# Splitting an output product around the end of its attention block: an adaptive-norm transformer block on one core

## The chip, the cores and the metric

The kernel runs on one core of a Trainium2 chip. The metric is the device time of one launch in microseconds (us). A core has five engines with a queue of instructions each, worked off in order: TensorE (PE in the profile; PEld is its weight load), VectorE (DVE), ScalarE (ACT), GpSimd (POOL) and SyncE (SP), which here issues all DMAs.

## The reference

One transformer block with conditioned norms on 2048 rows of 512: a modulation row from a condition vector, full softmax attention with 32 heads of 16, and a feed-forward part of width 1792 with the Mish function.

```python
mod = (_silu(c) @ w_mod).reshape(c.shape[0], 6, 1, -1)
sa, ca, ga, sb, cb, gb = (mod[:, 0], mod[:, 1], mod[:, 2], mod[:, 3], mod[:, 4], mod[:, 5])
h = _layernorm(x, axis=-1) * (1 + ca) + sa
x = x + ga * _A_ref(h, A_wqkv, A_wo)      # attention: softmax(q k^T / 4) v, then @ wo
h = _layernorm(x, axis=-1) * (1 + cb) + sb
x = x + gb * _B_ref(h, B_w1, B_b1, B_w2)  # mish(h @ w1 + b1) @ w2
return x
```

Everything is fp32. Operands of the large products are held as a rounded high part and a low part ("h" and "l"), and a product is three products (high x high, high x low, low x high) summed in one bank.

## The kernel before

The rows are cut into 4 blocks of 512 queries (`NB`), the heads into 8 groups of 4 (`G`); an iteration `n` is one group of one block, 32 in all, and it has 16 *steps*, so the loop has `T` = 512 steps. The code counts in half steps `h` (two to a step); `at(h, f)` puts work at a half step, and each engine's instructions are then issued in that order. Nothing is scheduled on the chip: a late engine makes those that wait for it late.

In a step TensorE makes four score tiles (keys x queries, L513, whose exponential ScalarE takes at L521), four tiles for the row maxima of an iteration 20 steps ahead (L472, reduced by VectorE at L474), and the product of the exponentials with the values (L541, eight records a step). Scores and maxima use one half of TensorE's rows at a time, and beside them, in the other half, run products of other work in *slots*: at first the q, k, v projections, later the MLP. Each such product is done in two halves, in the even and the odd step of a pair. `next_part` takes the next *unit* from the list `units` at an even step, if its time `ready` has come; 6 slots go into a step pair, so a unit of 12 takes two pairs (8 half steps) and one of 6 takes one pair (4 half steps). In the last 20 steps, which have no maxima, 3 slots go into a pair's step. A unit accumulates in the one bank `ms`; its `fin` evicts it.

The row maxima of a group go through `max_rows` (L485 on): transposed, negated into `mt` by ScalarE (L494), reduced to their rounded rows `mh` by GpSimd (L495), subtracted by GpSimd (L496), and written by DMA beside the queries, where the score product subtracts them.

When the 8 groups of a block are through (the last one's rows are normalized by GpSimd at L587 and split at L96 and L99 into `o_hl`), the block's MLP work starts, beside the next block's attention. For blocks 0 to 2 the queue is, in this order (`all_blocks`): the last down units of the block before, the output product `wo` of the four row tiles (12 slots each, not before half step `t0` = 256 (qb + 1) + 14), the norm (`norm_y`) and the transposes of the four tiles (`tr_unit`, a *special* that is put at a step's end), and 14 `up` units (the first MLP product with `mish` behind it, 12 slots) mixed with `down` units (the second MLP product, in 5 groups of 2, 4, 4, 2 and 2 of the 14 slices, each for 4 row tiles, 6 or 12 slots). Block 0 can only begin when the projections are through and the MLP's memory is open.

After an output product ScalarE copies the bank into `yd` (L824; one buffer), GpSimd adds it to the rows `y`, which hold x (L825), ScalarE sums the rows for the mean (L702), takes the squares (L706), and GpSimd makes the norm (L703 to L709). `tr_unit` evicts the transposed tile with ScalarE (L851), scales it with GpSimd (L854) and splits it into `hx` (L96, L99). `down` units evict in the same way (L896, L897).

Block 3 has no attention to hide behind: `tail` does its MLP alone, with full-height products. The third block's last ten down units are held back (`mst["held"]`) and fill TensorE in the tail while the last rows are normed on VectorE (L1023 to L110) and transposed (L1045). Their additions to y are VectorE's (L893).

```python
for js in ((0, 1), (2, 3)):
    for f in held(js):
        f(None)
...
fins = held((4, 5))
```

Of the kernel before, what the change touches and what calls it, by code (L numbers as in the profile page):

```python
# [18 lines left out]
def adaln_block(ctx: ExitStack, tc: tile.TileContext, x, wqkv, wo, w1, b1, w2, c, w_mod, out):  # L19
    nc = tc.nc  # L20
# [60 lines left out]
    nc.vector.tensor_scalar_mul(lows[:32], lows[:32], -1.0)  # L81
    modc = cst.tile([P, 4, DK], F32, name="modc")
    sil = cst.tile([P, DK], F32, name="sil")
# [227 lines left out]
    with ExitStack() as es:  # L311
# [36 lines left out]
        def stats_tb(tb):  # L348

            mv = lp.tile([P, 4, 2], F32, tag="ln_mv4", name="ln_mv4", bufs=2)  # L350
            rs = rss[tb] = lp.tile([P, 4, 4], F32, tag="ln_rs4", name="ln_rs4", bufs=3)
# [5 lines left out]
            nc.gpsimd.tensor_scalar(rs[:, 3, :], mv[:, :, 0], -1.0, 0.0, op0=ALU.mult, op1=ALU.add)  # L357
            nc.gpsimd.tensor_tensor(rs[:, 1, :], rs[:, 0, :], nhalf.to_broadcast([P, 4]), op=ALU.pow)
            nc.gpsimd.tensor_mul(rs[:, 2, :], rs[:, 3, :], rs[:, 1, :])
# [126 lines left out]
    def max_rows(n, mm):  # L486
        t = ring(2)
        cols = mm.rearrange("p a v q -> p (a v q)")
        for g in range(2):
            r = slice(64 * g, 64 * g + 64)  # L490
            nc.tensor.transpose(t[:32, g, :64], cols[r], ident[r, r])
        mh, mt = [ap.tile([32, P], F32R, tag=n_, name=n_, bufs=1) for n_ in ("mh", "mt")]
        mc = mt.bitcast(F32)
        nc.scalar.activation(mc.rearrange("p (g q) -> p g q", g=2), t[:32, :, :64], AF.Copy, scale=-1.0)  # L494
        nc.gpsimd.tensor_scalar_mul(mh, mc, lows[:32])  # L495
# [200 lines left out]
    def norm_y(y):  # L696
        mp = mst["p"]
        xn = mp.tile([P, D], F32, tag="hb", name="xn2", bufs=3)
        ss = mp.tile([P, 4], F32, tag="ln_s", name="ln_s", bufs=4)

        def mean():
            nc.scalar.activation(xn, y, AF.Identity, accum_out=ss[:, 0:1])  # L702
            nc.gpsimd.tensor_scalar(ss[:, 1:2], ss[:, 0:1], -1.0 / D, 0.0, op0=ALU.mult, op1=ALU.add)  # L703

        def spread():
            nc.scalar.activation(xn, y, AF.Square, bias=ss[:, 1:2], accum_out=ss[:, 2:3])  # L706
            nc.gpsimd.tensor_scalar(ss[:, 2:3], ss[:, 2:3], 1.0 / D, EPS, op0=ALU.mult, op1=ALU.add)
            nc.gpsimd.tensor_tensor(ss[:, 3:4], ss[:, 2:3], nhalf, op=ALU.pow)
            nc.gpsimd.tensor_scalar(xn, y, ss[:, 1:2], ss[:, 3:4], op0=ALU.add, op1=ALU.mult)  # L709

        return xn, mean, spread
# [85 lines left out]
    def block(qb, t0):  # L797

        xn, y, act, w1s, w2s, wos, done, hx = {}, {}, {}, {}, {}, {}, {}, []
# [14 lines left out]
        def wo_unit(i, tag):  # L814
# [3 lines left out]
            seq = [(l[:, k, s], wos[k][:, v, :]) for k in range(DK) for l, v in ((oh, 0), (oh, 1), (ol, 0))]  # L818
# [3 lines left out]
            def fin(h):  # L822
                yd = mst["p"].tile([P, D], F32, tag="yd", name="yd", bufs=1)
                nc.scalar.copy(yd, acc)  # L824
                nc.gpsimd.tensor_add(y[i], yd, y[i])  # L825

                def mean():
                    xn[i], first, then = norm_y(y[i])
                    first()
                    at(h + 5, then)  # L830

                at(h + 3, mean)
                done["xn", i] = h + 7
# [47 lines left out]
        def down_unit(gi, i, tag=None, acc=None):  # L881
# [9 lines left out]
            def fin(h):  # L891
# [24 lines left out]
                if then and (gi, i) == (4, 0):  # L916
                    load(h + 20, then["y"], lambda j: load_y(qb + 1, j), range(3, 4))
# [3 lines left out]

        def wo(i):
            queue(lambda: max(t0, done.get("w", 0 if qb else 4 * T)), lambda tag: wo_unit(i, tag))
            queue_special(lambda: done.get(("xn", i), 4 * T), lambda: tr_unit(i))
# [9 lines left out]
        if qb == NB - 2:  # L934
            mst["held"] = lambda j, acc: down_unit(2 + (j + 2) // 4, (j + 2) % 4, None, acc)
        return {"wo": wos, "y": y, "w1": w1s, "w2": w2s, "loads": first_loads,
                "units": {"wo": wo, "up": up, "down": down}}

    def all_blocks():
# [3 lines left out]
        for qb, b in enumerate(blocks):  # L943
            wo, up, down = (b["units"][k] for k in ("wo", "up", "down"))
            before = blocks[qb - 1]["units"]["down"] if qb else lambda gi, i: None
            before(4, 0)
            for i in range(4):
                wo(i)
# [17 lines left out]
            up(13)  # L966
            if qb < NB - 2:
                down(2, 2)
                down(2, 3)
# [24 lines left out]
    def tail():  # L994
# [46 lines left out]
        fins = held((4, 5))  # L1041
# [8 lines left out]
        for js in ((6, 7), (8, 9)):  # L1050
# [329 lines left out]
```

## Time and profile before

| | us |
|---|---|
| median of 3 runs (lowest, highest) | 1688.13 (1687.86, 1689.64) |
| the profiled execution's own time | 1686.03 |
| its span, first to last instruction | 1684.2 |
| TensorE busy | 1655.4 |
| VectorE busy | 1427.3 |
| ScalarE busy | 1327.9 |
| GpSimd busy | 928.3 |

Busy times are sums over the span, and the engines work at the same time. The rows of the profile name a line, an engine, an operation, what it writes and reads, how often it comes, then busy time and mean duration in ns, then idle time in front of it and who ended that. The timeline's rows begin with start and duration in us; the bracket is idle time in front and its releaser. The granted clock of TensorE was 0.998 over the span.

### The profile page before, as it was taken

The numbers are of one execution on the slowest core, as the hardware profiler recorded it, in microseconds if no ns is written. First come the engines' busy times: TensorE is split into PE (matmuls) and PEld (weight loads), VectorE is DVE, ScalarE is ACT, GpSimd is POOL, SyncE is SP. The second block draws the span as 40 slices with busy tenths as digits, with TensorE's granted clock in tenths as the row PEclk, the third lists the DMA queues.
The fourth block names the chain that finished last, engine by engine and source line by source line (L and its number), as shares of the span: only waits on it lengthen the run. The fifth ranks groups of instructions, "written<-read, shape, count | busy, mean of one in ns | idle before, by whom it ended". The sixth has DMA issues, their size and how long they took to land.

```text
span 1684.2 us, 33102 instructions
## 1 busy us (share of the span) xinstructions
PE 1655.4 (98%) x12316; PEld 925.5 (55%) x12316; DVE 1427.3 (85%) x2330; ACT 1327.9 (79%) x2591; POOL 928.3 (55%) x970
## 2 busy tenths in 40 slices
PE   7999999999999999999999999999999999999999
PEld 5755665555435455555555555555555555554687
DVE  6898898888898888888888888888888888882577
ACT  6257777787778889888889898888888888889364
POOL 5156225465435398854535498654535597645532
PEclk9999999999999999999999999999999999999999
DMA  7777456777784343435343644334442644232362
GB/s 256 191 221 213 123 158 195 236 227 218 213 249 113 107 107 86 119 78 161 87 122 75 199 104 97 102 108 118 122 102 59 189 103 133 80 122 83 126 225 75
DMA packets 113993, 240.04 MB, mean 143 GB/s; under 512 B 24048, under 2 KB 49648, under 8 KB 107784
## 3 DMA queue, kind: packets, MB, share of 16 engines
q1 hardware_dynamic: 113832, 237.92, 50.1%
q8 instruction: 97, 1.59, 0.4%
q14 instruction: 64, 0.52, 0.1%
HBM read 179.95 MB, written 51.44 MB: 137 GB/s over the span
## 4 chain that ended last, share of the span: by engine, by line
PE 84%; POOL 5%; DVE 3%; ACT 3%; issue 2%; DMA 2%; SPq 0%; POOLq 0%; ACTq 0%; DVEq 0%
PE bk L541 27%; PE ring L472 22%; PE ring L513 20%; PE bk L133 6%; PE bk L127 3%; PE ring L127 3%; ACT pr L521 2%; PE ring L1078 2%; DVE mx L474 1%; DMA ka<-kscr 1%; POOL rr L775 1%; POOL ee L773 1%; POOL hb L776 1%; POOL ee L743 1%; POOL hb L777 1%
## 5 line engine op out<-in xcount | busy, mean ns | idle before, releaser
L474 DVE TENSOR_REDUCE mx<-ring 128x1 f32<-128x512 f32 x2048 | 1279.2, 684 | 168.4 <-PE bk L133 110.6
L521 ACT ACTIVATE pr<-ring 128x512 f32<-128x512 f32 x2048 | 1088.0, 604 | 210.4 <-PE bk L133 164.4
L472 PE MATMUL ring<-ka,qa 64*128 64x512 f32 x2048 | 775.1, 426 | 1.7 <-DVE mx L474 0.7
L513 PE MATMUL ring<-qa,ka 64*128 64x512 f32 x2048 | 719.4, 395 | 5.7 <-ACT pr L521 5.2
L472 PEld LDWEIGHTS ring<-ka,qa 64*128 64x128 f32 x2048 | 365.9, 184 | 412.8 <-DVE mx L474 354.2
L541 PE MATMUL bk<-pr,vg 128*32 128x512 f32 x4096 | 545.1, 604 | 0.0
L513 PEld LDWEIGHTS ring<-qa,ka 64*128 64x128 f32 x2048 | 374.1, 184 | 112.1 <-ACT pr L521 40.2
L133 PE MATMUL bk<-h,w 64*128 64x512 f32 x1008 | 281.2, 409 | 0.0
L133 PE MATMUL bk<-w,a_h 64*128 64x512 f32 x576 | 194.7, 417 | 2.6 <-ACT pr L521 1.2
L133 PEld LDWEIGHTS bk<-h,w 64*128 64x128 f32 x1008 | 171.6, 184 | 2.4 <-ACT yd L896 0.4
L541 PEld LDWEIGHTS bk<-pr,vg 128*32 128x32 f32 x4096 | 80.9, 108 | 124.7 <-issue 116.7
L133 PE MATMUL bk<-w,a_l 64*128 64x512 f32 x288 | 113.8, 395 | 0.0
L743 POOL TENSOR_SCALAR ee<-hb 128x512 f32<-128x512 f32 x42 | 62.4, 1486 | 91.9 <-ACT hb L737 83.1
L133 PEld LDWEIGHTS bk<-w,a_h 64*128 64x128 f32 x576 | 95.3, 185 | 7.5 <-ACT pr L521 2.4
L773 POOL TENSOR_TENSOR ee<-ee,rr 128x512 f32<-128x512 f32 x42 | 53.8, 1282 | 71.8 <-ACT rr L764 71.6
L133 PE MATMUL bk<-w,o_hl 64*128 64x512 f32 x288 | 79.6, 408 | 0.0
L99 POOL TENSOR_TENSOR a_l<-hb,a_h 128x512 fp32r<-128x512 f32 x53 | 71.6, 1351 | 4.4
L897 POOL TENSOR_TENSOR y<-yd,y 128x512 f32<-128x512 f32 x40 | 51.4, 1286 | 28.2 <-ACT yd L896 28.2
L495 POOL TENSOR_SCALAR mh<-mt,lows 32x128 fp32r<-32x128 f32 x32 | 19.1, 596 | 81.4 <-ACT mt L494 81.2
L133 PE MATMUL bk<-h_h,wl 64*128 64x512 f32 x168 | 56.8, 418 | 0.0
L777 POOL TENSOR_TENSOR hb<-hb,rr 128x512 f32<-128x512 f32 x42 | 54.5, 1298 | 3.3
L758 POOL TENSOR_TENSOR ee<-ee,rr 128x512 f32<-128x512 f32 x42 | 54.0, 1286 | 3.5
(210 smaller groups left out, 1852.5 us busy)
## 6 DMA issues: line engine op xcount, KB each, us to landing
ka<-kscr SPq DMA_DIRECT2D x124, 384.0 KB
w<-w2scr SPq DMA_DIRECT2D x56, 512.0 KB
w<-w1scr SPq DMA_DIRECT2D x46, 512.0 KB
vg<-vscr SPq DMA_DIRECT2D x32, 552.0 KB
qa<-qscr SPq DMA_DIRECT2D x124, 100.0 KB
kscr<-qh SPq DMA_DIRECT2D x16, 512.0 KB
qscr<-qh SPq DMA_DIRECT2D x32, 256.0 KB
w1scr<-hl SPq DMA_DIRECT2D x14, 512.0 KB
```

The source lines that it names most:

```text
L99: (nc.gpsimd if eng == "p" else nc.vector).tensor_sub(lo, src, hi.bitcast(F32))
L127: nc.tensor.matmul(acc, l, r, start=start, stop=stop)
L133: i = nc.tensor.matmul(acc, l[64 * g:64 * g + 64], r[64 * g:64 * g + 64], start=start, stop=stop)
L472: nc.tensor.matmul(pm, qt[64 * s:64 * s + 64, qs * P:(qs + 1) * P], kt[64 * s:64 * s + 64, kb * TB:(kb + 1) * TB], start=True, stop=True)
L474: return nc.vector.tensor_reduce(out=mxs[n][:, s, 4 * j + qs, kb:kb + 1], in_=pm, op=ALU.max, axis=AX.X)
L513: nc.tensor.matmul(p_, kt[64 * s:64 * s + 64, kc * P:(kc + 1) * P], qt[64 * s:64 * s + 64, :], start=True, stop=True)
L521: e = nc.scalar.activation(pr, p_, AF.Exp, scale=SCALE)
L541: nc.tensor.matmul(accs[n][32 * h:32 * h + 32, :], vgs[n][:, o:o + 32], pts.pop((t, h)), start=(kc == 0), stop=(kc == 15))
L743: nc.gpsimd.tensor_scalar_min(buf("ee", 2), b["hb"], HCAP)
L758: nc.gpsimd.tensor_mul(ee, ee, rr)
L773: nc.gpsimd.tensor_mul(ee, ee, rr)
L777: nc.gpsimd.tensor_mul(hb, hb, rr)
```

## The change

The output product of a row tile becomes two units of 6 slots: `part` with the first two of the four slices of the contraction (heads 0 to 15, which are through long before the block's end) and `wo` with the other two. The four parts stand in the queue behind the first of the previous block's last down units and in front of the four `wo`, and need not wait for `t0`. Both halves are copied to `yd` and added to `y`.

The mean of a row is no longer summed over `y`: it is the mean of x, kept from the first norm in `xmean`, plus the two copies' own sums (`accum_out`). The squares come 3 half steps behind the eviction instead of 5.

In `max_rows`, ScalarE makes `mh` from the transposed bank, with a per-partition scale; GpSimd keeps the subtraction.

The third block's down(2,2) and down(2,3) leave the tail for the loop, so that 8 down units are held instead of 10; 5 of them, not 6, stand ahead of the transposes. The fourth row tile's x for the next block is loaded 11 half steps behind down(4,0) instead of 20.

```diff
-        nc.gpsimd.tensor_scalar_mul(mh, mc, lows[:32])
+        nc.scalar.activation(mh.rearrange("p (g q) -> p g q", g=2), t[:32, :, :64], AF.Identity, scale=lows[:32])
         nc.gpsimd.tensor_add(mt, mc, mh.bitcast(F32))
...
-        def mean():
-            nc.scalar.activation(xn, y, AF.Identity, accum_out=ss[:, 0:1])
-            nc.gpsimd.tensor_scalar(ss[:, 1:2], ss[:, 0:1], -1.0 / D, 0.0, op0=ALU.mult, op1=ALU.add)
...
-            seq = [(l[:, k, s], wos[k][:, v, :]) for k in range(DK) for l, v in ((oh, 0), (oh, 1), (ol, 0))]
+            seq = [(l[:, k, s], wos[k][:, v, :]) for k in ks for l, v in ((oh, 0), (oh, 1), (ol, 0))]
...
             def fin(h):
                 yd = mst["p"].tile([P, D], F32, tag="yd", name="yd", bufs=1)
-                nc.scalar.copy(yd, acc)
+                if ks[0] == 0:
+                    ss[i] = mst["p"].tile([P, 4], F32, tag="ln_s", name="ln_s", bufs=4)
+                m, part = (ss[i][:, j:j + 1] for j in ((0, 2) if ks[0] == 0 else (1, 3)))
+                nc.scalar.activation(yd, acc, AF.Identity, accum_out=part)
                 nc.gpsimd.tensor_add(y[i], yd, y[i])
-                def mean():
-                    xn[i], first, then = norm_y(y[i])
-                    first()
-                    at(h + 5, then)
-                at(h + 3, mean)
-                done["xn", i] = h + 7
+                nc.gpsimd.tensor_scalar(m, part, -1.0 / D, 0.0, op0=ALU.mult, op1=ALU.add)
+                if ks[0] == 0:
+                    nc.gpsimd.tensor_add(m, m, xmean[:, 4 * qb + i:4 * qb + i + 1])
+                    return
+                nc.gpsimd.tensor_add(m, m, ss[i][:, 0:1])
+                def spread():
+                    xn[i] = norm_y(y[i], ss[i])
+                at(h + 3, spread)
+                done["xn", i] = h + (7 if i else 5)
...
-                    load(h + 20, then["y"], lambda j: load_y(qb + 1, j), range(3, 4))
+                    load(h + 11, then["y"], lambda j: load_y(qb + 1, j), range(3, 4))
...
+        def part(i):
+            queue(lambda: 0 if qb else done.get("w", 4 * T) + 4, lambda tag: wo_unit(i, tag, range(2)))
+
         def wo(i):
-            queue(lambda: max(t0, done.get("w", 0 if qb else 4 * T)), lambda tag: wo_unit(i, tag))
+            queue(lambda: t0, lambda tag: wo_unit(i, tag, range(2, DK)))
...
-            mst["held"] = lambda j, acc: down_unit(2 + (j + 2) // 4, (j + 2) % 4, None, acc)
+            mst["held"] = lambda j, acc: down_unit(3 + j // 4, j % 4, None, acc)
...
             before(4, 0)
+            for i in range(4):
+                b["units"]["part"](i)
             for i in range(4):
                 wo(i)
...
             up(13)
+            down(2, 2)
+            down(2, 3)
             if qb < NB - 2:
-                down(2, 2)
-                down(2, 3)
...
-        fins = held((4, 5))
+        fins = held((4,))
...
-        for js in ((6, 7), (8, 9)):
+        for js in ((5, 6), (7,)):
```

More of the change, by code (lines that the diff above doesn't have):

```diff
@@ L80, in adaln_block @@
                             axis=AX.XY)
-    nc.vector.tensor_scalar_mul(lows[:32], lows[:32], -1.0)
     modc = cst.tile([P, 4, DK], F32, name="modc")
+    xmean = cst.tile([P, NKC], F32, name="xmean")
     sil = cst.tile([P, DK], F32, name="sil")
@@ L350, in stats_tb @@
             mv = lp.tile([P, 4, 2], F32, tag="ln_mv4", name="ln_mv4", bufs=2)
-            rs = rss[tb] = lp.tile([P, 4, 4], F32, tag="ln_rs4", name="ln_rs4", bufs=3)
+            nm = xmean[:, 4 * tb:4 * tb + 4]
+            rs = rss[tb] = lp.tile([P, 3, 4], F32, tag="ln_rs4", name="ln_rs4", bufs=3)
             for i in range(4):
@@ L694, in load_y, with norm_y @@
         return y
[L696 to L699, printed above, removed]
-        def mean():
[L702 to L711, printed above, removed]
+    def norm_y(y, ss):
+        xn = mst["p"].tile([P, D], F32, tag="hb", name="xn2", bufs=3)
+        nc.scalar.activation(xn, y, AF.Square, bias=ss[:, 1:2], accum_out=ss[:, 2:3])
+        nc.gpsimd.tensor_scalar(ss[:, 2:3], ss[:, 2:3], 1.0 / D, EPS, op0=ALU.mult, op1=ALU.add)
+        nc.gpsimd.tensor_tensor(ss[:, 3:4], ss[:, 2:3], nhalf, op=ALU.pow)
+        nc.gpsimd.tensor_scalar(xn, y, ss[:, 1:2], ss[:, 3:4], op0=ALU.add, op1=ALU.mult)
+        return xn
     def put_h(hh, hl, acc, k, tail):
@@ L797, in block @@
     def block(qb, t0):
-        xn, y, act, w1s, w2s, wos, done, hx = {}, {}, {}, {}, {}, {}, {}, []
+        xn, y, ss, act, w1s, w2s, wos, done, hx = {}, {}, {}, {}, {}, {}, {}, {}, []
         def load(h, d, load_, keys):
@@ L934, in block @@
         if qb == NB - 2:
-            mst["held"] = lambda j, acc: down_unit(2 + (j + 2) // 4, (j + 2) % 4, None, acc)
+            mst["held"] = lambda j, acc: down_unit(3 + j // 4, j % 4, None, acc)
         return {"wo": wos, "y": y, "w1": w1s, "w2": w2s, "loads": first_loads,
-                "units": {"wo": wo, "up": up, "down": down}}
+                "units": {"wo": wo, "part": part, "up": up, "down": down}}
     def all_blocks():
```

6 lines of the change are left out of this document (3 added, 3 removed).

## The prediction

> **What bounds the kernel now.** I read the page first, then TensorE's timeline around a few steps, then a table of stretches, then the groups by line, and at last the timelines of GpSimd, ScalarE and VectorE where a step was longer than its neighbours.
>
> ```profile
> span 1684.2 us, 33102 instructions
> PE 1655.4 (98%) x12316; PEld 925.5 (55%) x12316; DVE 1427.3 (85%) x2330; ACT 1327.9 (79%) x2591; POOL 928.3 (55%) x970
> PE 84%; POOL 5%; DVE 3%; ACT 3%; issue 2%; DMA 2%; SPq 0%; POOLq 0%; ACTq 0%; DVEq 0%
> ```
>
> TensorE is busy nearly always and carries 84% of the chain; GpSimd is the only other engine with a share worth a look. But a busy TensorE is not one price per step. The loop's 512 steps each end with eight records of the values' product (L541), so the starts of two such groups are one step apart:
>
> ```profile
> 457.22 1.06 PE L541 MATMUL bk<-pr,vg 128*32 128x512 f32 x8
> 459.95 1.06 PE L541 MATMUL bk<-pr,vg 128*32 128x512 f32 x8
> ...
> 840.54 1.07 PE L541 MATMUL bk<-pr,vg 128*32 128x512 f32 x8
> 842.62 0.49 PE L133 MATMUL bk<-w,a_h 64*128 64x512 f32 x1 [0.58 <-ACT yd L896]
> 844.52 1.06 PE L541 MATMUL bk<-pr,vg 128*32 128x512 f32 x8
> ```
>
> ```profile
> 457.22:468.17 10.95, 10.29 (x68) 4.07 (x67) 10.14 (x18) 8.38 (x18) 0.88 (x2) 1.00 0.72 256
> 504.37:515.75 11.38, 11.38 (x93) 6.14 (x91) 10.27 (x18) 9.63 (x21) 2.52 (x4) 1.00 0.36 137
> 1528.00:1537.00 9.00, 9.00 (x67) 3.94 (x65) 0.93 (x2) 8.84 (x18) 8.67 (x10) 1.00 0.56 211
> ```
>
> (Columns: stretch, its length, busy time and count on PE, PEld, DVE, ACT, POOL, then clock and DMA.) The first stretch is four steps without MLP products: 10.95 / 4 = 2.74 us, and VectorE is busy 10.14 of it, four maxima of 0.68 us a step. The second is four steps with six products: 11.38 / 4 = 2.845 us, TensorE full. So six product slots, which keep TensorE busy, cost 0.11 us a step as long as VectorE needs 2.74 us anyway. The third stretch lies in the last 20 steps, which have no maxima: ScalarE is busy 8.84 of 9.00 us there, and the steps last about 2.1 us. Above these floors stand a few longer steps, such as 840.54 to 844.52 (3.98 us, 1.14 too long). After the loop comes a tail in which TensorE works alone.
>
> **The tail: two product units less.** By the queue's order (the times follow from the units' lengths, 12 slots two step pairs, 6 slots one), the second block's units follow the first's without a gap, and so do the third's: each block waits neither for its start time nor for the attention, except block 0, which stands idle from half step 232 to 272. There the four first parts take half steps 252 to 268, the second parts end at 288 instead of 304, and everything behind moves forward by 16 half steps, through blocks 1 and 2. At the end this makes room for down(2,2) and down(2,3) of the third block, which end exactly with the loop, in 16 steps at three slots. In the tail these are 24 products fewer:
>
> ```profile
> 1583.77 11.17 PE ring L127 x48
> 1596.68 5.58 PE ring L127 x24
> ```
>
> ```profile
> 1590.26 0.55 DVE L110 TENSOR_SCALAR pr<-pr,ln_mv,ln_rs 128x512 f32<-128x512 f32 x1 [0.72 <-POOL ln_rs L108]
> 1590.72 2.47 DVE L893 TENSOR_TENSOR y<-ring,y 128x512 f32<-128x512 f32 x4
> 1594.77 0.60 PE L1045 MATMUL ring<-ident,pr 128*128 128x128 f32 x4
> ```
>
> One product is 11.17 / 48 = 0.233 us, so 24 are 5.6 us. But the 48 before the transposes (L1045) also covered the norm of the last rows, which ends at 1590.8 (L110). Now there are 30, which end at 1583.4 + 7.0 = 1590.4. The first transposes take the bank that VectorE's first y addition frees, at about 1590.72 + 0.68 = 1591.4: one microsecond of wait appears, of which the 18 products behind the transposes (4.2 us against 5.6) hide what the splits of h need. I take 0.7 us back: **-4.9 us**, bounds -5.6 (all) and -3.8.
>
> In the last 20 steps the slots are free, since ScalarE sets them. The price in the loop is block 0's gap: 8 steps at 2.845 instead of 2.74, **+0.8 us**.
>
> **GpSimd: one small operation less in 32 groups, and a shift of the blocks against the attention.**
>
> ```profile
> L495 POOL TENSOR_SCALAR mh<-mt,lows 32x128 fp32r<-32x128 f32 x32 | 19.1, 596 | 81.4 <-ACT mt L494 81.2
> L494 ACT ACTIVATE mt<-ring 32x128 f32<-32x128 f32 x32 | 8.3, 259 | 5.9 <-PE ring L491 3.6 <-issue 1.7 <-ACT pr L521 0.6
> ```
>
> ```profile
> 608.86 0.59 POOL L495 TENSOR_SCALAR mh<-mt,lows 32x128 fp32r<-32x128 f32 x1
> 610.07 1.49 POOL L743 TENSOR_SCALAR ee<-hb 128x512 f32<-128x512 f32 x1
> ...
> 833.66 0.60 POOL L495 TENSOR_SCALAR mh<-mt,lows 32x128 fp32r<-32x128 f32 x1 [8.38 <-ACT mt L494]
> 834.75 1.26 POOL L773 TENSOR_TENSOR ee<-ee,rr 128x512 f32<-128x512 f32 x1
> 840.67 1.28 POOL L897 TENSOR_TENSOR y<-yd,y 128x512 f32<-128x512 f32 x1
> ```
>
> ```profile
> 611.59 0.63 ACT L749 ACTIVATE ee<-ee 128x512 f32<-128x512 f32 x1 [0.86 <-POOL ee L743]
> ```
>
> The long step at 840.54 is GpSimd's: maxima (833.66) stand in front of unit 13's quotient (834.75 on), that in front of the y addition (840.67 to 841.95), ScalarE's next copy into the single buffer yd waits for this addition, and TensorE for the copy (842.62). The same comes in block 1, at 1212. With the blocks 16 half steps earlier, half a group, the maxima no longer fall there: the 1.1 us in front go, and with them nearly the whole wait: 2 x 1.1 = **-2.2 us** (bounds 0 and -2.3). At 611.59 ScalarE stands 0.86 us for a clamp that waited behind mh (608.86), and such steps come as a pair in each block; of the three pairs' 3.7 us over the floor I take **-2.2 us** (0, if other work takes the place of the maxima, to -3.7).
>
> ScalarE gets 32 more small operations. By L494 each is 0.26 us, 8.3 us in all. In steps of 2.845 us it is busy 9.63 / 11.38, some 0.4 us free per step, so most are hidden; in the last 20 steps one is not. I take **+0.9 us** (0 to +4, half of the 8.3 us, if banks come free later). The Trainium skill, "ScalarE: Activation LUTs", section "What ACT_TABLE_LOAD costs", says that a per-partition pointer operand adds about 93 ns to an activation; the new one has such a scale and L494 has none. By that it would be 0.35 us, 11.3 us in all, an estimate, and the sum above would be 0.1 us higher for the one that is not hidden.
>
> **The output product in two parts.** ScalarE's work is neutral:
>
> ```profile
> L824 ACT COPY yd<-bk 128x512 f32<-128x512 f32 x12 | 7.1, 591 | 0.0
> L702 ACT ACTIVATE xn<-y 128x512 f32<-128x512 f32 x10 | 6.2, 624 | 0.0
> L702 ACT ACTIVATION_READ_ACCUMULATOR xn<-y 128x1 f32 x10 | 1.9, 194 | 0.0
> L706 ACT ACTIVATE xn<-y,ln_s 128x512 f32<-128x512 f32 x10 | 7.3, 726 | 0.0
> ```
>
> Twelve copies and twelve mean passes (0.59 + 0.62) become 24 copies with sums (L702's price, twice). GpSimd gets 12 more y additions and 36 more tiny ones. What matters is the pace: the four tiles now come every 4 half steps (two steps, 5.7 us) instead of every 8.
>
> ```profile
> 887.77 1.28 POOL L825 TENSOR_TENSOR gate<-yd,gate 128x512 f32<-128x512 f32 x1 [1.38 <-ACT yd L824]
> 889.27 1.73 POOL L854 TENSOR_SCALAR hf<-hf,modc 128x128 f32<-128x128 f32 x4 [0.22 <-PE bk L133]
> 891.09 0.62 POOL L96 TENSOR_SCALAR h<-hf 128x512 fp32r<-128x512 f32 x1
> 891.79 1.29 POOL L99 TENSOR_TENSOR h<-hf,h 128x512 fp32r<-128x512 f32 x1
> 893.64 0.19 POOL L703 TENSOR_SCALAR ln_s<-ln_s 128x1 f32<-128x1 f32 x1 [0.56 <-ACT xn L702]
> 896.66 0.19 POOL L707 TENSOR_SCALAR ln_s<-ln_s 128x1 f32<-128x1 f32 x1 [2.84 <-ACT xn L706]
> 896.94 0.56 POOL L708 TENSOR_TENSOR ln_s<-ln_s,nhalf 128x1 f32<-128x1 f32 x1
> 897.61 0.77 POOL L709 TENSOR_SCALAR xn<-gate,ln_s 128x512 f32<-128x512 f32 x1
> ```
>
> One tile is 1.28 + 1.73 + 0.62 + 1.29 + 0.19 + 0.19 + 0.56 + 0.77 = 6.6 us; with the second tiny addition (0.19, or 0.56 if it is like L708) and the gaps it is 7.2. So GpSimd falls behind by 1.5 us a tile. Its cover is the three leftover down units before the first up: up(0) comes 24 half steps (34 us) after the first second part. Followed operation by operation, with a wait of 9 us before the first transposed tile, GpSimd is done with the last half of h at about 34.4 us. It just fits; I take 0.6 us a block for the Squares that find their mean late and for up(0). In block 0 GpSimd also prepares late weights there, and the last normalized attention rows come close:
>
> ```profile
> 495.39 1.28 POOL L99 TENSOR_TENSOR o_hl<-od,o_hl 128x512 fp32r<-128x512 f32 x1
> ```
>
> They are ready at 496.7, and TensorE now needs them in the first step pair, near 499, instead of the second; two of the new additions (1.7 us each) ahead of them would bring them to 500.1: 1.1 us. Together 1.1 + 3 x 0.6, rounded up: **+3.0 us**; bounds 0 and +13 (1.5 us for each of three blocks' four tiles would be 18, less some 5 of cover). No gain is left here that is not counted above.
>
> The parts stand ahead of everything in block 0, so their operands must be there. The group at 457.22 is step 121's, so half step 252 (step 126) begins near 457.22 + 4 x 2.74 + 1.06 = 469.2:
>
> ```profile
> 462.42 0.45 SPq L669 DMA_DIRECT2D w<-woscr  x1
> ```
>
> The second of the two weights that they need was issued at 462.4, 6.8 us earlier, and is used three slots into the step; I take no wait. Each part adds an eviction of the one MLP bank, and the next unit's products queue behind ScalarE's copy; the six-slot down units do the same already and keep 2.84 us a step (all but the ones named above): nothing. SyncE's y load is issued 9 half steps earlier and waits for the store of a row that was issued 3 half steps (4 us) before; behind it stand key and query loads with steps to spare: nothing. The negation that goes at the start and the mean column's new place cost nothing either.
>
> **The sum**: -4.9 + 0.8 - 2.2 - 2.2 + 0.9 + 3.0 = -4.6 us. The profiled execution took 1686.0 us (span 1684.2), which makes 1681.4; the median of the runs is 2.1 us above it, 1688.1, which makes **1683.5 us**.
>
> **The rivals.** *Slower: GpSimd bounds the output stage.* With tiles at 5.7 us and 7.2 us of work, 1.5 us of lag a tile reach TensorE through the Squares (ScalarE stands, the exponentials behind it, their banks). If two thirds of the lag arrive, 4 us in each of three blocks, 12 instead of 3, the sum is +4.4: 1692.5 us. It decides from about 2.5 us a block on. For it: ScalarE already stood for GpSimd at 611.59. Against: the leftover down units, and idle times such as 2.84 us before 896.66. Chance 0.14. *The stalls only move.* Half a group of shift brings the maxima and the attention's products into other places of GpSimd's queue, and the 4.4 us stay: -0.2, 1687.9 us. Chance 0.16. *The tail hides nothing more.* If norm, transposes and splits of h are what the tail waits for, the 5.6 us of products are replaced by idle TensorE, and -1.0 stays of it: 1687.4 us. Against it: the transposes came 4 us after the norm's end. Chance 0.10. *The parts do not go ahead* (weights or rows not landed at half step 252): then nothing shifts but the first block, and 8 steps of wait are at stake; about 1688. Chance 0.04.
>
> **How the numbers follow.** The forecast has 0.56, with an own range of 1680.5 to 1686.5. About 0.2% (3.4 us) is what a measurement of this kernel can tell from no change; 1684.7 is that line, so some 0.12 of the forecast's chance falls inside it. Faster 0.44 and 0.07 from the milder ends of the two middle rivals: 0.51; slower 0.14; the same 0.35. The range of 1680.0 to 1690.0 leaves out 0.1 on each side.
>
> **What would show it.** Right: eight records of L541 2.84 us apart from half step 252 on, TensorE's L127 group ahead of the transposes x30 and behind them x18, L1045 some 3.5 us nearer to the loop's end, no step of 3.98 us in front of blocks 1 and 2. Wrong: steps over 3.3 us between the second parts and up(0), ScalarE's Square or yd waiting for GpSimd by more than 2 us a block, or TensorE idle at the transposes for more than 2 us.

## The result, and the profile after

| | before | after |
|---|---|---|
| median of 7 runs each (lowest, highest), us | 1688.43 (1687.79, 1689.64) | 1694.1 (1692.3, 1695.46) |
| profiled execution, us | 1686.03 | 1692.3 |

The change is slower: the ratio of after to before is 1.0038, 95% interval 1.0029 to 1.0047. The forecast was 1683.5 us.

From the page of the kernel after, the span, the engines and the chain:

```profile
span 1690.5 us, 33209 instructions
PE 1656.9 (98%) x12340; PEld 927.9 (55%) x12340; DVE 1424.8 (84%) x2327; ACT 1336.2 (79%) x2637; POOL 934.8 (55%) x988
PE 89%; DMA 3%; DVE 3%; ACT 2%; POOL 2%; issue 1%; SPq 0%; ACTq 0%; DVEq 0%; POOLq 0%
```

TensorE has 1.5 us more work, the span 6.3 us more, and no engine's share moves by more than a point. The sums do not show where the time went; the steps do. I take the length of step s as the distance from one group of the values' product (L541 before, L542 after) to the next, and add it up by stage.

| stage | steps | before | after | difference |
|---|---|---|---|---|
| first part of the loop | 4 to 124 | 348.62 | 350.25 | +1.63 |
| block 0's output product and norm | 124 to 158 | 97.37 | 102.22 | **+4.85** |
| the rest of its MLP | 158 to 262 | 298.87 | 297.22 | -1.65 |
| block 1's output product and norm | 262 to 286 | 70.57 | 74.20 | **+3.63** |
| the rest of its MLP | 286 to 390 | 298.87 | 297.21 | -1.66 |
| block 2's output product and norm | 390 to 414 | 70.56 | 74.16 | **+3.60** |
| the rest of its MLP | 414 to 490 | 218.08 | 217.54 | -0.54 |
| last steps | 490 to 513 | 49.58 | 49.08 | -0.50 |
| tail, from the last L542 | | 114.92 | 110.66 | **-4.26** |

The differences add to 5.1 us; the other 1.2 us lie ahead of the loop. Neither that nor the +1.63 is shown to be the change's: from the span's start to step 124, the kernels below that are made from after took 466.9 to 471.3 us (after 468.2), one that changes only `mh` took 468.0, one that changes only the means 466.7, and before's profiled execution 465.4, which was a quick one: 2.4 us under the median of its seven runs. So the change gives 4.8 us in the tail and the last steps and 3.9 in the MLP stages, and takes 12.1 in the three output stages. That is 3.4 us of the 5.7 between the medians. After's profiled execution was itself 1.8 us under its median, and where its other runs lose that is not shown.

**The tail came as forecast.** From the chain of waits of the kernel after, and VectorE's and TensorE's timeline:

```profile
1603.71 4.20 PE ring L127 x18
```

```profile
1600.55 0.55 DVE L110 TENSOR_SCALAR pr<-pr,ln_mv,ln_rs 128x512 f32<-128x512 f32 x1 [0.72 <-POOL ln_rs L108]
1601.01 3.08 DVE L891 TENSOR_TENSOR y<-ring,y 128x512 f32<-128x512 f32 x5
1601.75 0.66 PE L1048 MATMUL ring<-ident,pr 128*128 128x128 f32 x4 [0.48 <-DVE y L891]
```

18 products behind the transposes, 30 ahead of them, and TensorE stands 0.48 us for VectorE's first y addition, the wait that the prediction named, at half its size. The transposes come 3.55 us nearer to the last L542.

**The output stage did not.** TensorE's timeline of the kernel after in block 1, its L542 records alone:

```profile
879.00 1.07 PE L542 MATMUL bk<-pr,vg 128*32 128x512 f32 x8
881.83 1.06 PE L542 MATMUL bk<-pr,vg 128*32 128x512 f32 x8
885.51 1.06 PE L542 MATMUL bk<-pr,vg 128*32 128x512 f32 x8
889.20 1.07 PE L542 MATMUL bk<-pr,vg 128*32 128x512 f32 x8
892.03 1.07 PE L542 MATMUL bk<-pr,vg 128*32 128x512 f32 x8
897.02 1.06 PE L542 MATMUL bk<-pr,vg 128*32 128x512 f32 x8
899.85 1.06 PE L542 MATMUL bk<-pr,vg 128*32 128x512 f32 x8
903.84 1.06 PE L542 MATMUL bk<-pr,vg 128*32 128x512 f32 x8
```

Before's, in the same steps (878.68 ends step 268 as 885.51 does above):

```profile
875.85 1.06 PE L541 MATMUL bk<-pr,vg 128*32 128x512 f32 x8
878.68 1.06 PE L541 MATMUL bk<-pr,vg 128*32 128x512 f32 x8
881.52 1.06 PE L541 MATMUL bk<-pr,vg 128*32 128x512 f32 x8
884.37 1.06 PE L541 MATMUL bk<-pr,vg 128*32 128x512 f32 x8
887.72 1.06 PE L541 MATMUL bk<-pr,vg 128*32 128x512 f32 x8
890.58 1.06 PE L541 MATMUL bk<-pr,vg 128*32 128x512 f32 x8
893.42 1.06 PE L541 MATMUL bk<-pr,vg 128*32 128x512 f32 x8
```

The second parts' evictions begin about here. Steps 268, 269, 271 and 273 (those that end at the L542 groups of 885.51, 889.20, 897.02 and 903.84) take 3.68, 3.69, 4.99 and 3.99 us. Before had 2.83, 2.84, 3.35 and 2.84 in their place. Its four steps with a transpose (271, 275, 279, 283) take 3.35 to 3.36, which is 2.84 and some 0.5 for the transpose itself; after's transposes are in 268, 271, 273 and 275. Block 2 repeats this step for step. In the windows of the kernel after and of before (columns: stretch, length, busy PE, PEld, DVE, ACT, POOL, clock, DMA, GB/s):

```profile
876.16:879.00 2.84, 2.84 (x24) 1.56 (x22) 2.49 (x5) 2.65 (x8) 1.65 (x3) 1.00 0.01 3
881.83:885.51 3.68, 3.68 (x32) 2.00 (x30) 3.41 (x6) 3.68 (x11) 3.09 (x6) 1.00 0.00 0
892.03:897.02 4.99, 3.55 (x32) 2.01 (x31) 3.67 (x6) 3.33 (x9) 3.68 (x8) 1.00 0.35 60
```

```profile
881.52:884.37 2.85, 2.85 (x25) 1.54 (x23) 2.55 (x5) 2.68 (x7) 0.19 (x1) 1.00 0.02 4
```

The first row is a step of after without a Square. In step 268 (the second row) ScalarE is busy 3.68 of 3.68 us; in a step of before with a Square (the last row) it was busy 2.68 of 2.85. In step 271 (the third row) TensorE is busy only 3.55 of 4.99. The timelines of ScalarE, GpSimd and TensorE tell why:

```profile
881.25 0.71 ACT L699 ACTIVATE xn<-y,ln_s 128x512 f32<-128x512 f32 x1
...
882.44 0.59 ACT L819 ACTIVATE yd<-bk 128x512 f32<-128x512 f32 x1
882.91 0.21 ACT L819 ACTIVATION_READ_ACCUMULATOR yd<-bk 128x1 f32 x1
883.01 3.04 ACT L522 ACTIVATE pr<-ring 128x512 f32<-128x512 f32 x6
...
895.28 0.72 ACT L699 ACTIVATE xn<-gate,ln_s 128x512 f32<-128x512 f32 x1 [0.89 <-POOL ln_s L825]
```

```profile
887.40 0.44 POOL L497 TENSOR_TENSOR mt<-mt,mh 32x128 fp32r<-32x128 f32 x1 [1.83 <-ACT mh L496]
887.90 1.75 POOL L852 TENSOR_SCALAR hf<-hf,modc 128x128 f32<-128x128 f32 x4
...
893.52 1.29 POOL L820 TENSOR_TENSOR gate<-yd,gate 128x512 f32<-128x512 f32 x1
894.78 0.19 POOL L821 TENSOR_SCALAR ln_s<-ln_s 128x1 f32<-128x1 f32 x1
895.05 0.19 POOL L825 TENSOR_TENSOR ln_s<-ln_s 128x1 f32<-128x1 f32 x1
```

```profile
887.85 0.50 PE L473 MATMUL ring<-ka,qa 64*128 64x512 f32 x1 [0.58 <-ACT hf L849]
896.63 0.46 PE L844 MATMUL ring<-ident,xn 64*128 64x64 f32 x7 [1.39 <-ACT pr L522]
```

Two things are mixed. At 881.25 stands the Square of one tile and at 882.44 the copy of the next, with one exponential between them; ScalarE does not pause until 886.05, and the step is simply too short for its work. In before a Square and the next copy lie 3.3 us apart:

```profile
883.78 0.71 ACT L706 ACTIVATE xn<-y,ln_s 128x512 f32<-128x512 f32 x1
...
887.10 0.59 ACT L824 COPY yd<-bk 128x512 f32<-128x512 f32 x1
```

In step 269 of after the copy of the first transposed tile stands behind `mt` and `mh` on ScalarE, and TensorE waits for it (887.85, 0.58 us). At 895.28 ScalarE stands 0.89 us for a mean that GpSimd makes at 895.05, because GpSimd worked without a pause from 887.40 on; the exponentials behind the Square are late, and with them the bank for the transpose (896.63, 1.39 us). The first is not in the prediction; the second resembles its slower rival. The experiments separate them.

### The profile page after: what moved, and what is told of

Same layout as the page of the kernel before. It is cut to its first block, busy times and chain, and to the rows that moved or that the text cites. A ratio compares the mean times of both kernels' runs of the same rounds, so it can differ in the third digit from the quotient of the medians.

```text
span 1690.5 us, 33209 instructions
## 1 busy us (share of the span) xinstructions
PE 1656.9 (98%) x12340; PEld 927.9 (55%) x12340; DVE 1424.8 (84%) x2327; ACT 1336.2 (79%) x2637; POOL 934.8 (55%) x988
## 4 chain that ended last, share of the span: by engine, by line
PE 89%; DMA 3%; DVE 3%; ACT 2%; POOL 2%; issue 1%; SPq 0%; ACTq 0%; DVEq 0%; POOLq 0%
PE bk L542 29%; PE ring L473 23%; PE ring L514 20%; PE bk L133 9%; PE bk L127 3%; PE ring L127 2%; PE ring L1081 2%; DVE mx L475 1%; ACT pr L522 1%; DMA ka<-kscr 1%; DMA qscr<-ql 1%; DMA wma<-in_w_mod 1%; DMA wr<-in_A_wqkv 0%; DMA xt<-in_A_x 0%; PE ring L844 0%
## 5 line engine op out<-in xcount | busy, mean ns | idle before, releaser
L542 PE MATMUL bk<-pr,vg 128*32 128x512 f32 x4096 | 545.1, 604 | 0.0
L133 PE MATMUL bk<-w,a_h 64*128 64x512 f32 x608 | 207.1, 419 | 0.9 <-ACT pr L522 0.8
L542 PEld LDWEIGHTS bk<-pr,vg 128*32 128x32 f32 x4096 | 80.9, 108 | 125.6 <-issue 117.6
L133 PE MATMUL bk<-w,a_l 64*128 64x512 f32 x304 | 119.4, 393 | 0.0
L765 POOL TENSOR_TENSOR ee<-ee,rr 128x512 f32<-128x512 f32 x42 | 53.9, 1283 | 98.2 <-ACT rr L756 97.9
L133 PEld LDWEIGHTS bk<-w,a_h 64*128 64x128 f32 x608 | 100.2, 184 | 3.7 <-ACT pr L522 1.8
L497 POOL TENSOR_TENSOR mt<-mt,mh 32x128 fp32r<-32x128 f32 x32 | 14.4, 450 | 92.3 <-ACT mh L496 92.3
L133 PEld LDWEIGHTS bk<-w,a_l 64*128 64x128 f32 x304 | 56.0, 184 | 3.6
L99 POOL TENSOR_TENSOR wl<-wr,wh 128x512 fp32r<-128x512 f32 (+1 forms) x13 | 17.7, 1365 | 70.7 <-ACT wh L92 70.6
```

Source lines behind the costliest of these rows:

```text
L99: (nc.gpsimd if eng == "p" else nc.vector).tensor_sub(lo, src, hi.bitcast(F32))
L133: i = nc.tensor.matmul(acc, l[64 * g:64 * g + 64], r[64 * g:64 * g + 64], start=start, stop=stop)
L542: nc.tensor.matmul(accs[n][32 * h:32 * h + 32, :], vgs[n][:, o:o + 32], pts.pop((t, h)), start=(kc == 0), stop=(kc == 15))
L765: nc.gpsimd.tensor_mul(ee, ee, rr)
```

## The experiments

Steps are numbered as in the table; the line numbers in a row are those of its own kernel, and differ a little from kernel to kernel. "Before" was run beside each kernel (medians 1687.2 to 1687.8 us); after was not run again, and its 1694.1 us is from the result above. Ratios are to before.

**One part of the change alone, and all but it: `mh` on ScalarE.** The kernel before with only this edit:

```diff
-    nc.vector.tensor_scalar_mul(lows[:32], lows[:32], -1.0)
...
-        nc.gpsimd.tensor_scalar_mul(mh, mc, lows[:32])
+        nc.scalar.activation(mh.rearrange("p (g q) -> p g q", g=2), t[:32, :, :64], AF.Identity, scale=lows[:32])
```

> The kernel before with that one part alone: ScalarE makes mh. If ScalarE's new operation costs, 1692 us or more. If it relieves GpSimd as the prediction took it (the 1.14 us at half steps 512 and 768 and the pairs of 0.6 and 0.5 us at 352 and 360, 608 and 616, 864 and 872), 1684.5 to 1687.5 us. Place and pace theories say the same of this one: the loss of the changed kernel is not in this part, so 1688.4 us or less.

Measured: 1684.9 us, 0.9983 (0.9974 to 0.9993): **faster than both kernels**. From its page, and the group of `mh` by lines:

```profile
PE 1653.7 (98%) x12316; PEld 923.9 (55%) x12316; DVE 1427.1 (85%) x2329; ACT 1334.6 (79%) x2623; POOL 910.8 (54%) x938
```

```profile
L494 ACT ACTIVATE mh<-ring,lows 32x128 fp32r<-32x128 f32 x32 | 11.0, 343 | 0.0
```

ScalarE makes `mh` in 0.34 us right behind `mt`, where GpSimd took 0.60 us and first had to come round to it. The MLP stages fall by 1.17, 1.24 and 0.90 us, the last steps by 0.45, the output stages by nothing (70.51, 70.57). The steps are 176, 304 and 432 (3.43 to 3.45, now 2.84 each), 256 and 384 (3.98 to 3.56) and 499 (3.64 to 3.05). The other way round, the kernel after with that line undone:

> The changed kernel with mh made by GpSimd again, as before. Theory that ScalarE's new operation is what costs: 32 operations of 0.34 us on a ScalarE that is 85% busy would be worth 4 to 6 us, 1688 to 1690 us. Place theory: it is worth 0.25 us in each of the three steps 269 and one in the last 20 steps, and GpSimd's 0.67 us a group come back as lateness in the steps that are 3.30 to 3.45 us around half steps 352, 608 and 864: no change or up to 2 us slower, 1693.5 to 1696 us. Pace theory: GpSimd has 0.6 us more in the output stage, slower by 0 to 2 us.

Measured: 1700.4 us, 1.0076 (1.0061 to 1.0091), 6.3 above after: 304 takes 4.01 instead of 3.30, 499 takes 3.66 instead of 3.04, 143, 271 and 399 some 0.6 more. That is more than any of the three expectations had. Steps 256 and 384 stay at 2.84 without `mh` on ScalarE, so the shift by itself removes their 3.98. This part is a gain alone and a larger one beside the split.

**The means from copies alone,** in the kernel before (copy of the whole product with `accum_out`, no pass over `y`):

> The kernel before with the means from the copies alone: undivided output product, one copy with its sum per tile, the Square 3 half steps behind it, mh on GpSimd as before. ScalarE loses a pass of 0.62 us per tile, 12 in all, in steps that mostly have room for it. Means harmless: 1686.5 to 1688 us (steps 410 and 282 at 2.84 instead of 3.05). If the tiny GpSimd operations or the earlier Square cost, 1689 us or more.

Measured: 1688.68 us, 1.0009 (1.0000 to 1.0018), 0.7 us over what was expected of a harmless edit; but the output stages are 70.60 and 70.63: it costs nothing there.

**The tail.** The kernel after with ten units held instead of eight:

```diff
-            mst["held"] = lambda j, acc: down_unit(3 + j // 4, j % 4, None, acc)
+            mst["held"] = lambda j, acc: down_unit(2 + (j + 2) // 4, (j + 2) % 4, None, acc)
...
```

> The changed kernel with down(2,2) and down(2,3) of the third block back in the tail, ten held units as before; the last steps' slots stay empty instead. The prediction priced the two units in the tail at 4.9 us (3.8 to 5.6): then this one takes 1698 to 1700 us, and its tail from the loop's end is as long as before's. If the tail hid them anyway, 1694 to 1695 us. If the last steps paid for them, it gains: under 1693 us.

Measured: 1698.3 us, 1.0065 (1.0046 to 1.0083), 4.2 above after; tail 117.39 instead of 110.66, last steps 46.57 instead of 49.08. The shift of two units is worth 4.2 us, so what eats it is elsewhere.

**The place of transposes and Squares.** First the first tile's transpose two half steps later, as for the others (`h + 7` for all):

> The changed kernel with one figure altered: the first row tile's transposes come 7 half steps behind its output product, as the other tiles' do, not 5. Place theory: the three output stages lose about 4 us each (in block 1 steps 268, 269, 271, 273 and 274 of the changed kernel's trace are 0.85, 0.84, 1.63, 1.15 and 0.48 us longer than before) because the first tile's transposes stand in the step of the row maxima (their two ScalarE operations then stand ahead of the transposes' copy) and ahead of the third tile's mean on GpSimd. Then this gives back 0.84 + 1.1 us a block, 5 to 6 us in all: about 1688.5 us, and steps 269 and 271 are back at 2.84 and 3.36 us. Pace theory: tiles every 4 half steps are too much for ScalarE and GpSimd wherever they stand; then the waits move by a step and the time stays at 1693 to 1695 us.

Measured: 1689.69 us, 1.0015 (1.0005 to 1.0025). Step 271 falls from 4.99 to 3.99, the stages of blocks 1 and 2 from 74.2 to 73.1: GpSimd's work on that tile no longer stands in front of the next mean, and no Square waits for GpSimd in this trace. But 271 was to come down to 3.36, and 269, where these transposes now stand, to 2.84; it takes 4.01. Then also the Square at `h + 4` instead of `h + 3`:

> The changed kernel with the transposes of the first tile at 7 half steps, as in the run before, and the Squares 4 half steps behind the output product, not 3. In that run each step with transposes still took 3.99 us where the kernel before takes 3.36; in it stand ScalarE's Square (0.71) and copy (0.59), and the transposes wait for the exponential behind them. Crowding theory: the Square in the step before leaves only the copy there; the three such steps of a stage come down to 3.4 to 3.5 us, 0.5 us each, 4 to 5 us in all against that run's 1689.7: 1685 to 1686 us. Rate theory: GpSimd's 7.2 us a tile at a tile per 6.2 us is what is late; the Square is only later by half a step, the normed rows too, and the transposes wait for GpSimd instead: 1689 to 1692 us.

Measured: 1689.98 us, 1.0013 (1.0004 to 1.0022), stages 72.6: another 0.4, and no more. The three steps with transposes do fall to 3.35 to 3.38 us, as the crowding theory had it, but 270 and 272 grow from 2.84 to 3.2 and 274 from 3.43 to 4.13: the crowding only moved. A different trouble shows in both, here in TensorE's timeline of the first of them:

```profile
473.87 0.50 PE L133 MATMUL bk<-w,o_hl 64*128 64x512 f32 x1 [0.77 <-DMA w<-woscr]
```

Step 126, block 0's first part, waits for its weights: it takes 5.33 us in this execution, 2.84 in that of after, and 2.8 to 4.6 in others. The third edit gives the weights four half steps more in block 0:

> As the run before it in this list, and block 0's parts start 4 half steps later (half step 256, still through by 272). In the profiles of the changed kernel and three variants half step 252 took 2.84, 5.33, 4.60 and 4.06 us, and the wait ends with the landing of the output weights. If that wait is real in most executions, this is worth 1 to 2 us against the run before it, and 252 is back at 2.74; if the loads only come later still (they are behind the same queue), nothing.

Measured: 1690.6 us, 1.0014 (1.0004 to 1.0025). The wait moves to step 128 (4.05), step 136 grows to 5.58, and nothing is gained.

**The pace.** The kernel after with second parts asked for every 8 half steps, and ten units held:

```diff
-            queue(lambda: t0, lambda tag: wo_unit(i, tag, range(2, DK)))
+            queue(lambda: t0 + 8 * i, lambda tag: wo_unit(i, tag, range(2, DK)))
```

> The changed kernel with the second parts 8 half steps apart, as the undivided units were, and ten held units in the tail again: the split alone, without its pace and without the shift of the blocks. Pace theories, both: the output stages lose nothing (22 steps of block 1's stage take 70 to 71 us as before, not 74.2), and the time is that of the kernel before with mh on ScalarE (1684.9) and the wait at half step 252: 1685 to 1687.5 us. If the split itself costs (24 evictions instead of 12, 12 more additions on GpSimd), 1689 us or more, with the stage at 72 us or more.

Measured: 1691.66 us, 1.0028 (1.0019 to 1.0037), and stages of 72.63 and 72.62 in blocks 1 and 2, as if pace did not matter. But there the edit did not bind: those start times were past when the units' turn came, and the copies still follow each other after two steps (889.63, 896.00, 902.80, 909.01 us). In block 0 it bound (copies in steps 137, 141, 145, 149), and that stage fell from 102.22 to 99.61. What blocks 1 and 2 show is something else: the second parts came six steps later than in after, behind the row maxima of step 269, and their stages fell by 1.6 us with a tile still every two steps or a little more. So it also matters what else falls into the stage; that was not taken apart. The pace had to be set by the order of the units, in blocks 1 and 2 (the first tile's transposes stand two half steps later there, as in the run above):

```diff
-                done["xn", i] = h + (7 if i else 5)
+                done["xn", i] = h + (7 if i or qb else 5)
...
                 b["units"]["part"](i)
+                if qb:
+                    wo(i)
             for i in range(4):
-                wo(i)
+                if not qb:
+                    wo(i)
```

> The kernel after, but in the second and third blocks each first part is followed at once by its second part (order part 0, wo 0, part 1, wo 1, ...), so that a finished row tile comes every four steps as in the kernel before, with the same units in the same total time; the first block is as after. Steps 262 to 286 (stage of the second block): 70.57 us before, 74.20 after. Theory 'pace' (a tile's work on ScalarE or GpSimd doesn't fit into two steps): the stage falls to 70.6 to 71.2 and step 390 to 414 too, the first block's steps 124 to 158 stay near 102, the tail near 110.7; time 1694.1 - 2 x 3.3 = 1687.5 us (1686.5 to 1688.5). Rival 'the split itself' (24 evictions with sums in place of 12, 48 more small GpSimd operations): the work is the same, so the stage stays at 73 to 74 and the time at 1693 to 1694.

Measured: 1695.31 us, 1.0049 (1.0032 to 1.0066): the time was missed by 8 us, and the stages came half way, to 72.20 and 72.31. The time first. I had overlooked that a second part must wait for its attention (`t0`): the first one now holds up the parts behind it, block 1's first up unit is evicted in step 287 instead of 281, and at the end the two units moved into the loop find no room. TensorE's timeline at the last step:

```profile
1578.59 0.73 PE L127 MATMUL bk<-w,a_h 128*128 128x512 f32 x2 [0.68 <-ACT yd L894]
1583.58 2.36 PE L1016 MATMUL bk<-ka,o_hl 128*128 128x512 f32 x9 [0.73 <-ACT yd L894]
```

MLP products still run at the loop's end, the last step takes 3.97 instead of 0.86, and the tail 113.99 instead of 110.66. The stage next. ScalarE's timeline of this kernel, and the window of step 268:

```profile
881.08 0.71 ACT L699 ACTIVATE xn<-y,ln_s 128x512 f32<-128x512 f32 x1
...
882.26 0.60 ACT L819 ACTIVATE yd<-bk 128x512 f32<-128x512 f32 x1
882.74 0.21 ACT L819 ACTIVATION_READ_ACCUMULATOR yd<-bk 128x1 f32 x1
882.83 3.04 ACT L522 ACTIVATE pr<-ring 128x512 f32<-128x512 f32 x6
```

```profile
881.66:884.89 3.23, 3.23 (x25) 1.57 (x23) 2.96 (x6) 3.23 (x10) 2.73 (x4) 1.00 0.00 0
```

Exponentials that follow each other start 0.48 us apart (six are through in 3.04 us), so the four of a step need 1.9 and leave about 0.9 of 2.84. Square (0.71) and copy with sum (882.26 to 882.83, 0.57) follow each other with one exponential between them, 1.28 us in one step's time, 0.4 over what is free; the step takes 3.23, 0.4 more than 2.84, with ScalarE busy all through. The same comes in 272, 276 and 280 (3.22, 3.22, 3.13).

**ScalarE or GpSimd: leaving work out.** Two runs of the kernel after, each with less work for one engine. In the first the Square goes over 64 of the 512 columns, in the second only one of four scale operations on h is made:

```diff
-        nc.scalar.activation(xn, y, AF.Square, bias=ss[:, 1:2], accum_out=ss[:, 2:3])
+        nc.scalar.activation(xn[:, :64], y[:, :64], AF.Square, bias=ss[:, 1:2], accum_out=ss[:, 2:3])
```

> The kernel after with the Square pass over 64 of 512 columns (the variance is of those columns alone, so the numbers it gives are others): ScalarE's work on a row tile in the output stage falls from 0.57 (copy with sum) + 0.71 (Square) + 0.5 (copy of the transposed tile) = 1.8 us to about 1.35, GpSimd's stays. Four exponentials of 0.515 us leave 2 x (2.84 - 2.06) = 1.56 us in two steps. Theory 'ScalarE is full': the stage of steps 262 to 286 falls from 74.2 to 72 or less, the same in block three, the first block from 102.2 to about 100; time about 1688 (1686 to 1690). Rival 'GpSimd falls behind': its 7.2 us a tile stay, the stage stays at 73.5 to 74.2, time 1692.5 to 1694.

Measured: 1688.16 us, 1.0007 (0.9997 to 1.0017); a Square takes 0.34 instead of 0.71 us, the stages fall to 73.08 and 73.04 (271 to 4.55, 273 to 3.62, 268 to 3.36).

```diff
-                for k in range(DK):
+                for k in range(1):
                     nc.gpsimd.tensor_scalar(hf[:, k], hf[:, k], modc[:, 3, k:k + 1], modc[:, 2, k:k + 1],
```

> The kernel after with one of the four GpSimd scale operations on each transposed row tile (three quarters of h stay unscaled): GpSimd's work on a tile falls from 7.2 to 5.9 us, near the 5.7 us in which a tile comes; ScalarE's stays. Theory 'GpSimd falls behind': the stage of steps 262 to 286 falls from 74.2 to 71.5 or less, the first block by as much, time about 1686 (1685 to 1688). Theory 'ScalarE is full': the stage stays at 73.2 to 74.2, time 1692 to 1694.

Measured: 1689.72 us, 1.0010 (1.0000 to 1.0020), stages 73.19 and 73.20. Of block 1's long steps only 271 changes, from 4.99 to 3.99, and no Square waits for GpSimd any more; 268, 269 and 273 stay at 3.67, 3.69, 3.99. Neither theory gets both its numbers (73.19 lies at the lower edge of what the ScalarE theory had, the time does not): less work on either engine is worth 1.0 to 1.1 us a block, so both are at work, and each alone leaves more than two thirds of the 3.6 us. (In both runs the time fell by more than the stages did, 5.9 and 4.4 us against 2.9 and 3.0 in all three stages; the start is another 0.9 us shorter in their traces and the MLP stages 0.6 to 0.8, and the rest is not accounted for.)

**Everything kept apart.** The kernel after with a tile every four steps in all blocks (order as in the alternating run, block 0 by start times), every transpose at `h + 7`, the Square at `h + 2`, between two evictions, and ten units held, as there is no room. In blocks 1 and 2 the place of the Square is the only new edit, and the second parts are evicted in about the same steps as in the alternating run:

```diff
-                at(h + 3, spread)
+                at(h + 2, spread)
...
```

> The kernel after with the two parts kept, but a finished row tile every four steps in all three blocks, as in the kernel before (block 0: second parts started 8 half steps apart; blocks 1 and 2: part 0, wo 0, part 1, wo 1, ...), every transpose at +7, the Square at +2 half steps after an eviction instead of +3, so that it lies between two evictions and not in the step of the next one, and ten units held for the tail as in the kernel before (no room is gained at that pace). Theory 'ScalarE has 0.78 us free in a step (2.84 less four exponentials of 0.515) and pays for what is over it': copy with sum (0.57), Square (0.71) and copy of the transposed tile (0.5) now lie in steps of their own; steps 268, 272, 276, 280, which were 3.22 us in the alternating run, go back to 2.84 to 2.95, the stage of steps 262 to 286 comes to 70.6 to 71.1 us (before 70.57, after 74.20), steps 124 to 158 to 98 to 99.5 (before 97.37, with 0.8 of it for the products in steps that were without any), the tail to 115; time 1686.5 (1685.5 to 1688). Rival 'the split itself costs' (12 evictions and 48 small GpSimd operations more): the stage stays at 72 or more, time 1690 or more.

Measured: 1688.04 us, 1.0003 (0.9993 to 1.0013), stages 70.80 and 70.83, block 0's 98.79, as expected. The time lies at the upper end (the part ahead of step 124 took 468.9 us in its trace). The tail is 117.17 where 115 was expected, and the last steps are 2.6 shorter than before's, 46.98. The window of step 268, where the copy (from 879.35) finds the Square (from 877.45) already done in the step before, and the L542 records on either side of it:

```profile
879.42:882.26 2.84, 2.84 (x24) 1.57 (x22) 2.78 (x6) 2.67 (x8) 2.31 (x4) 1.00 0.00 0
```

```profile
879.44 1.06 PE L542 MATMUL bk<-pr,vg 128*32 128x512 f32 x8
882.26 1.07 PE L542 MATMUL bk<-pr,vg 128*32 128x512 f32 x8
```

ScalarE is busy 2.67 of 2.84 us and the step has its floor again, with every extra eviction and every small GpSimd operation of the split still there.

## Why the prediction was wrong, and where it was right

**The step that failed** is the term "+3.0 us" for the output product in two parts. Without block 0's gap (0.8, counted apart) it measured 4.85 + 3.63 + 3.60 - 0.8 = 11.3 us, 8.3 more than that. Of the signs of being wrong that the prediction named, steps over 3.3 us between the second parts and the first up came; Squares that wait for GpSimd by over 2 us a block did not (0.89 us, once a block). Inside the term, the 1.1 us for block 0's attention rows were about right (step 136 is 0.79 longer; TensorE waits for `o_hl`); the 0.6 us a block for everything else was 3.3 to 3.6.

It failed at two sentences. "ScalarE's work is neutral" compares totals: 24 copies with sums for 12 copies and 12 passes. The total is neutral, but the pace was doubled, and I applied the pace to GpSimd alone. From start to start in the timelines, a tile costs ScalarE 0.57 + 0.71 + 0.5 = 1.8 us (copy with sum, Square, copy of the transposed tile), which is all that two steps leave (2 x 0.9); one step leaves 0.9, and the code puts a Square and a copy, 1.28, into one step's time. And "each part adds an eviction ... nothing" took the down units as proof, most of which evict into steps without a Square. Before had one place in blocks 1 and 2 where a down unit's copy (917.79) and a Square (919.70) come close together: step 282, and 128 steps later 410, of 3.05 us each. Beside these two, the 0.6 us for Squares that find their mean late was too small: GpSimd's lag costs 1.0 to 1.1 us in blocks 1 and 2.

The 3.63 us of block 1, by runs that each make one more edit there: with the first tile's transposes later, 74.20 becomes 73.06 (1.1; no Square waits for GpSimd any more, and less work for GpSimd alone gives nearly the same, 73.19); with a tile every four steps 72.20 (0.9 more); with the Square moved away from the copy 70.80 (1.4); before had 70.57, so the split itself costs 0.2. In block 2 the stages are 74.16, 73.10, 72.31, 70.83 and 70.56. Each share is that of the edit in this order; with a tile every two steps, moving the Square (there half a step later) gave only 0.4. What part of block 0's 4.05 us is which was not taken apart; its pace alone was worth 2.6 (99.61).

**The rival** "GpSimd bounds the output stage" had nearly the size, 12 us and 1692.5, and the result is near its time. Its mechanism, however, carries about 1.1 of block 1's 3.6 us, and not as a lag that grows by 1.5 us with every tile: once the first tile's transposes come later, the same work at the same pace lets no Square wait. So it was right by its sum and not by its reason.

**Right:** the tail (-4.9 forecast; -4.26 measured, and 4.2 by the run that undoes it; the -0.50 of the last steps lies in step 499, where `mh` on ScalarE alone gives as much); the shift, since the up units of blocks 0 to 2 are evicted 8 steps (16 half steps) earlier than before; the two steps of 3.98 us (both 2.84 now, -1.14 each); and that the pairs of steps would give part of their 3.7 us. All MLP stages together with that came to -3.85, where the prediction had -2.2 - 2.2 + 0.9 = -3.5. That sum was right by errors that cancel: ScalarE's `mh` was booked as a cost of 0.9 and is a gain of 2.7 on its own; some of the other gains were its, and new small waits came with the shift (steps 193, 321 and 449, +0.44 to +0.48). In the trace of after `mh` is 0.34 us where `mt` is 0.26. That is close to the about 0.09 us for a pointer operand that the Trainium skill, "ScalarE: Activation LUTs", section "What ACT_TABLE_LOAD costs", states, and it made no difference.

**Weights for the first part** were near the edge, as the 0.04 rival feared: no wait in the profiled execution of after, 1.2 to 2.5 us at step 126 in five of the other ten kernels that hold the split. How often that happens in untraced runs of after stays open.

## What to carry to other kernels

When a change makes a stage's work come faster, divide each engine's work on an item by the new interval, for every engine and not for the one under suspicion, and then look at which operations share one step: here some 0.9 us were free, and 1.28 us were put into it. A share of 79% over the span, or an unchanged total, says nothing of that. And take a bundle of edits apart: the smallest one here, 32 operations of 0.6 us moved off a busy queue, was, of the two tried alone, the one that paid, and by itself it beats both kernels (1684.9 us).

## What the runs showed of the hardware

The accumulator read of an activation with a sum lasts 0.18 to 0.21 us in the rows of after (882.91), but the next activation starts 0.10 us behind its start (883.01), and exponentials of 0.6 us that follow each other start 0.48 apart (six in 3.04 us). Busy times of single rows thus overstate what ScalarE needs; room in a step is better read from starts.
